# Packed attention and mixture of experts: the first batches' tokens in long pieces, turned by TensorE, and shorter fillers

## The chip, the cores and the metric

One core of a Trainium2 chip. The metric is the device time of one execution in microseconds; of several runs the median counts.

## What is computed

Eight batches of 576 tokens, eight heads of 64. In each head 32 packs attend to the keys, and the queries then attend to the packed result. Its output, heads side by side, goes through a mixture of eight experts with one expert per token.

```python
p_packed = sm_attn(p, k, v)                 # (8, 8, 32, 64)
x = sm_attn(q, p_packed, p_packed)          # (8, 8, 576, 64) -> (8, 576, 512)
logits = np.einsum('bsd,de->bse', x, w_gate)
local_gate = 1.0 / (1.0 + np.exp(-np.einsum('bsd,de->bse', x, w_local).squeeze(-1)))
...
if s == 0 or local_gate[b, s] < 0.5: e = fresh_e      # argmax of the logits
else: e = prev_e
...
h = np.maximum(x[b, s] @ w1[e], 0.0)
out[b, s] = p[e] * (h @ w2[e])
```

## The kernel before

The kernel reads from token 0 of each batch which expert that batch uses and runs the whole batch through it; a part behind a branch mends the tokens for which that doesn't hold, and isn't entered with these inputs. For each batch there is attention (scores of packs against keys, packs, queries against packs), then the choice of the expert (line 565), a register read on SP (line 568), the loads of that expert's w1 and w2 (lines 721 and 730), the product of packs and w1 (line 747), and two layers in eight chunks (lines 770 and 809 to 818). The attention weights go into layer 1 in two parts, a2h and a2l (lines 532 and 535).

Everything is unrolled. The order of the instructions on all engines is written out when the program is built: each piece of work is a generator, `weave` steps one of them at a time, and a model of the engines (`Clock`) says when its inputs, buffers and PSUM banks will be there. `price` holds the model's durations. `need(...)` gives the earliest time of the next step; `weave` takes loads first, then attention work of the earliest batch, then the layers (`main`), weighed by a credit. An attention step may be put ahead of the time at which ScalarE and VectorE are done with their queue by a limit: twice the limit for a step that takes PSUM banks, once for other steps of batches up to `soon`, and none for later batches. `soon` is the first batch whose expert isn't chosen yet. All engines work in the order that results; SP issues nearly all DMAs in order, and one that must wait for a buffer holds up those behind it.

Batch 0 is special (`early`). Its keys and values are loaded as tokens: 96 partitions, pieces of 1536 bytes (`load_tokens`, line 270), in four buffers `kv`. VectorE turns the keys (line 344) in blocks of 32x32. Queries of all batches, and the keys of batches 1 to 7, are loaded in blocks (`load_blocks`, line 284): 128-byte pieces, four transfers, in three buffers `qn`, and VectorE turns them in place (lines 465 and 353). Batch 0's queries are turned after its expert is chosen. Batch 1's loads stand in the order values, packs (line 301), keys, queries; the keys wait until two of batch 0's w2 blocks have been issued, the queries until four have.

Until the first layer starts, TensorE also gets fillers (line 210): products of a constant tile, 128x128 by 256 columns, whose result isn't used. Five stand at the start; one is added for each 450 ns that the model sees TensorE wait, and one whenever the model's share of matmul work falls under a half (`BUSY`, `SLACK`). PSUM has six banks for attention work until then and three afterwards.

Lines that the steps below speak of: scores 385, softmax of the scores 392 to 417, their transposes 427, packs 439 and 454, early choice 577 to 606, query matmuls 480, their softmax 498 to 526, packed weights 747 to 757.

Of the kernel before, what the change touches and what calls it, by code (L numbers as in the profile page):

```python
# [21 lines left out]
HQ = 4  # L22
NQ = H // HQ
TP = 96
# [14 lines left out]
WARM, BUSY, SLACK = 5, 0.5, 1500.0  # L39
# [9 lines left out]
FIRST_W2 = {"k": 2, "q": 4}  # L49
# [5 lines left out]
class Clock:  # L55
# [3 lines left out]
    def __init__(self):  # L59
        self.until, self.written, self.used, self.before = {}, {}, {}, {}  # L60
        self.slots, self.done, self.group, self.tiled, self.products, self.work = {}, set(), (None, set()), False, 0.0, 0.0

        self.rate = 300.0

# [18 lines left out]
    def ready(self, tiles):  # L83
        return max((self.written.get(x.tensor.name, (0.0, None))[0] + LAT for x in tiles), default=0.0)
# [4 lines left out]
    def price(self, inst, outs, ins):  # L89
        kind = str(inst.engine).split(".")[-1]  # L90
        n = max(x.free_size() for x in outs + ins)
        psum = any(x.space == PSUM for x in ins)
        if kind == "PE":
            n = outs[0].free_size()
            rows, at = outs[0].partition_size(), outs[0].start_partition()
            tiled = min(ins[0].partition_size(), rows) <= 64 and rows != 64
            full = n * (0.833 if inst.is_transpose else 1.667 if ins[0].dtype == F32 else 0.4167) + (3 if tiled else 15)

            shape, cell = (rows, n, ins[0].partition_size()), (ins[0].start_partition(), at)
            beside = rows < 128 and shape == self.group[0] and cell not in self.group[1]  # L100
# [6 lines left out]
            self.products += 27.0 if beside else full  # L107
            if not inst.is_transpose:
                self.work += 27.0 if beside else full
            return kind, 27.0 if beside else full  # L110
        extra = len(outs) - 1 + sum(x.free_size() == 1 and n > 1 for x in ins)
        if kind == "Activation":
            return kind, 0.833 * n + (51 if psum else 93) + 93 * extra
        if kind == "DVE" and inst.opcode == "Reciprocal":
            return kind, 6.3 * n + 65
        if kind == "DVE":
            return kind, 1.042 * n + 65 + 60 * extra
        return kind, 1.92 * n + 100

    def note(self, inst):  # L120
# [14 lines left out]
        for x in ins + ([] if dma else outs):  # L135
            at, by = self.written.get(x.tensor.name, (0.0, kind))
            start = max(start, at + (LAT if by != kind else 0.0 if kind == "PE" else SAME))
        for x in outs:
            t = x.tensor.name
            start = max(start, 0.0 if dma else self.used.get(t, 0.0))  # L140
            if t in self.before:
                start = max(start, self.used.get(self.before.pop(t), 0.0) + LAT)
# [4 lines left out]
        for x in ins:  # L147
            self.used[x.tensor.name] = max(end, self.used.get(x.tensor.name, 0.0))
        for x in outs:
            self.written[x.tensor.name] = (end, kind)  # L150
            self.used[x.tensor.name] = max(end, self.used.get(x.tensor.name, 0.0))
# [3 lines left out]
def packed_attn_moe_kernel(  # L155
# [46 lines left out]
    warm = const.tile([128, 256], F32, name="warm")  # L202
# [5 lines left out]
    def keep_warm(n):  # L208
        for _ in range(n):
            nc.tensor.matmul(out=warm_ps[:, :256], lhsT=warm[:, :128], rhs=warm, start=True, stop=True)  # L210
# [41 lines left out]
    def need(*tiles, slot=(), banks=0, when=None):  # L252
# [10 lines left out]
        ready.banks = banks  # L263
# [40 lines left out]
    def begin(b, st, early=False):  # L304
        st["b"], st["early"] = b, early
        st["gate"] = gate_all[b % 3 if isinstance(b, int) else 0]
        st["ppT"] = [None] * NQ
        st["quads"] = st["asked"] = st["scored"] = st["weighed"] = st["raised"] = 0

    def loads(st):  # L310

        b = st["b"]
        if st["early"]:
# [7 lines left out]
            order = (("k", 0), ("k", 1), ("v", 0), ("v", 1), ("q", 1))  # L321
        else:
            if isinstance(b, int):
                yield need(when=lambda: "loaded" in sts[b - 1] and (b < 2 or "ereg" in sts[b - 2]))
            order = (("v", 0), ("v", 1), ("p", 1), ("k", 1), ("q", 1))
        for name, Q in order:
            blocks = name == "q" or (name == "k" and not st["early"])
            if isinstance(b, int) and b == 1 and name in FIRST_W2:
                yield need(when=lambda: len(sts[0].get("w2", ())) >= FIRST_W2[name])
# [15 lines left out]

    def turn_keys(st, Q):

        if not st["early"]:
# [18 lines left out]
    def scores(st, Q):  # L367
# [10 lines left out]
        yield need(key, st["p"], banks=n)  # L378
# [21 lines left out]
        if st["scored"] == NQ:  # L400
# [6 lines left out]
        chunks = sc.rearrange("a (x r p) -> a x r p", x=J3, r=2) if st["early"] \  # L407
            else sc.rearrange("a (r p x) -> a x r p", r=2, x=J3)
# [52 lines left out]
    def turn_queries(st, Q):  # L461
        yield need(when=lambda: "q" in st and "a2t" in st and (not st["early"] or "ereg" in st))
        yield need(st["q"])
        qT = st["q"].rearrange("a (h q) x -> a q h x", q=NQ)[:, Q]
        nc.vector.transpose(out=qT, in_=qT)  # L465
        st["qT", Q] = qT

    def queries(st, Q):

        yield need(when=lambda: st["ppT"][Q] is not None and ("qT", Q) in st and (not st["early"] or ("qT", 1 - Q) in st))  # L470
# [4 lines left out]
        yield need(ppq, st["q"], banks=2)  # L475
# [49 lines left out]
        for r in range(2):  # L525
            nc.vector.transpose(
                out=a2t.rearrange("a (m r) -> a r m", r=2)[:, r],
                in_=sT[:, r].rearrange("a m n -> a (m n)"),
            )
# [182 lines left out]
    def weights(st):  # L712
# [49 lines left out]
    def layer1(c, half, st):  # L762
# [5 lines left out]
        for Q in range(NQ):  # L768
            for wi, ai in ((0, 0), (0, 1), (1, 0)):
# [143 lines left out]
    def weave(main):  # L913
# [3 lines left out]
        idle, seen = SLACK, (START, 0.0)  # L917
        while main in threads or any(x.batch < 0 for x in threads):
# [4 lines left out]
            while started < B and started <= max(at_batch[0], 0) + AHEAD:  # L923
# [3 lines left out]
                    turn_keys(st, 0), turn_keys(st, 1), scores(st, 0), scores(st, 1), keys(st, 0), keys(st, 1), gate_weights(st) if started == 0 else None, gates(st), turn_queries(st, 0), turn_queries(st, 1), queries(st, 0), queries(st, 1),  # L927
# [5 lines left out]
            if at_batch[0] < 0:  # L933
# [8 lines left out]
            behind = max(clock.engine("Activation"), clock.engine("DVE"))  # L942
# [127 lines left out]
```

## Time and profile before

| | us |
|---|---|
| median of 3 runs | 443.4 |
| lowest and highest | 442.42, 444.82 |
| the profiled execution | 446.23 |
| its span, first to last instruction | 444.5 |
| TensorE busy | 424.1 (95%) |
| VectorE, ScalarE, GpSimd busy | 309.1, 176.4, 24.5 |
| first layer-1 matmul of batch 0 | 41.28 |
| first layer-1 matmul of batch 1 | 100.44 |

DMA moved 73.15 MB in 179381 packets, 151424 of them under 512 bytes. The page gives the shares over the whole span; windows give them by stage. In a timeline a line is a run of like instructions: start, length, engine, source line, operation, output and inputs, count, and in brackets the idle time before it and what ended it. PEclk is the granted clock of TensorE as a share of 2.4 GHz: 0.50 is 1.2 GHz.

### The profile page before, as it was taken

What the parts mean: (1) busy time and instruction counts of PE and PEld (TensorE: products, weight loads), DVE (VectorE), ACT (ScalarE), POOL (GpSimd) and SP (SyncE); (2) the same over time, 40 slices, a digit from 0 to 9 for tenths busy, and PEclk for the clock granted to TensorE, in tenths of its full rate; (3) what the DMA queues carried; (4) which work ended last, traced back from release to release, by engine and by line L of the source; (5) the groups of instructions that cost most, each with busy time, mean ns of one, the idle gap of its engine ahead of it and who ended that gap; (6) DMA issues with size and microseconds to landing.
All of it is one profiled execution on the core that took longest, in us unless ns stands there. A gap on an engine that the chain in (4) does not pass through costs nothing.

```text
span 444.5 us, 9978 instructions
## 1 busy us (share of the span) xinstructions
PE 424.1 (95%) x3860; PEld 329.2 (74%) x3861; DVE 309.1 (70%) x837; ACT 176.4 (40%) x400; POOL 24.5 (6%) x41
## 2 busy tenths in 40 slices
PE   8788899979999999999999999999999999999993
PEld 6565587837787678768886778678876888778882
DVE  4478658874897669857986788758985588544331
ACT  1305233345252644355433453445334443344222
POOL 0000000200011001100020002000110002000000
PEclk9888899978999999999999999999999999999998
DMA  9999999999974999399949993799946120821003
GB/s 189 151 245 194 161 217 138 92 324 203 132 161 141 330 133 176 111 323 153 148 164 355 145 165 119 264 198 149 211 137 219 45 88 1 315 106 65 1 1 112
DMA packets 179381, 73.15 MB, mean 165 GB/s; under 512 B 151424, under 2 KB 158336, under 8 KB 179328
## 3 DMA queue, kind: packets, MB, share of 16 engines
q1 hardware_dynamic: 177200, 72.30, 77.9%
q8 instruction: 32, 0.52, 0.6%
q10 hardware_dynamic: 2128, 0.15, 0.4%
q14 instruction: 21, 0.17, 0.2%
HBM read 63.00 MB, written 9.44 MB: 163 GB/s over the span
## 4 chain that ended last, share of the span: by engine, by line
PE 81%; DVE 6%; DMA 4%; SPq 3%; issue 2%; ACT 1%; POOLq 0%; POOL 0%; DVEq 0%
PE acc L809 38%; PE bank L770 22%; PE bank L747 3%; PE bank L439 3%; PE acc L814 3%; PE acc L818 3%; SPq L284 2%; PE bank L427 2%; DVE qn L353 2%; PE bank L480 2%; PE bank L385 2%; DMA p_in<-in_p_dram 2%; DMA qn<-in_k_dram 2%; DMA kv<-in_k_dram 1%; DVE h L785 1%
## 5 line engine op out<-in xcount | busy, mean ns | idle before, releaser
L809 PE MATMUL acc<-w2s,h 128*128 128x512 f32 x768 | 209.1, 403 | 0.0
L809 PEld LDWEIGHTS acc<-w2s,h 128*128 128x128 f32 x768 | 136.2, 190 | 31.6 <-issue 8.6
L780 ACT ACTIVATE h<-bank 128x288 fp32r<-128x288 f32 x128 | 52.7, 412 | 123.3 <-PE bank L770 113.5
L785 DVE SCALAR_TENSOR_TENSOR h<-bank,h 128x288 fp32r<-128x288 f32 (+2 forms) x192 | 61.3, 346 | 43.4 <-ACT h L780 42.5
L770 PE MATMUL bank<-a2h,wph 128*128 128x288 f32 x256 | 78.3, 306 | 2.6 <-DVE df L680 1.2
L770 PE MATMUL bank<-a2h,wpl 128*128 128x288 f32 x256 | 76.1, 297 | 0.0
L770 PE MATMUL bank<-a2l,wph 128*128 128x288 f32 x256 | 75.6, 295 | 0.0
L770 PEld LDWEIGHTS bank<-a2h,wph 128*128 128x128 f32 x256 | 48.4, 189 | 18.7 <-issue 7.3
L770 PEld LDWEIGHTS bank<-a2l,wph 128*128 128x128 f32 x256 | 48.6, 190 | 4.5
L798 DVE TENSOR_TENSOR w2s<-w2raw,w2s 128x512 fp32r<-128x512 f32 x64 | 47.1, 736 | 3.1 <-ACT w2s L796 2.8
L770 PEld LDWEIGHTS bank<-a2h,wpl 128*128 128x128 f32 x256 | 48.5, 189 | 0.0
L796 ACT CAST w2s<-w2raw 128x512 fp32r<-128x512 f32 x64 | 39.4, 615 | 1.2 <-DMA w2raw<-in_moe_w_dram 1.0
L535 POOL TENSOR_TENSOR a2l<-a2t,a2h 128x576 fp32r<-128x576 f32 x14 | 20.5, 1465 | 329.9 <-ACT a2h L532 329.9
L757 DVE TENSOR_TENSOR wpl<-bank,wph 128x512 fp32r<-128x512 f32 x30 | 19.3, 683 | 16.0 <-ACT wph L754 16.0
L814 PE MATMUL acc<-w2s,h 128*128 128x512 f32 x64 | 26.2, 410 | 0.0
L818 PE MATMUL acc<-w2s,h 128*64 128x512 f32 x64 | 25.3, 395 | 0.0
L210 PE MATMUL acc<-warm 128*128 128x256 f32 x78 | 23.9, 469 | 1.2 <-DVE warm L203 1.2
L754 ACT CAST wph<-bank 128x512 fp32r<-128x512 f32 x30 | 16.1, 590 | 21.3 <-PE bank L747 21.3
L210 PEld LDWEIGHTS acc<-warm 128*128 128x128 f32 x78 | 18.1, 240 | 5.7 <-issue 1.6
L465 DVE STREAM_TRANSPOSE qn<-qn 128x1152 f32<-128x1152 f32 x16 | 21.8, 1368 | 0.1
L353 DVE STREAM_TRANSPOSE qn<-qn 128x1152 f32<-128x1152 f32 x14 | 19.0, 1358 | 2.4 <-DMA qn<-in_k_dram 2.4
L447 DVE TENSOR_SCALAR zz<-bank,rs 128x128 f32<-128x128 f32 x16 | 5.6, 351 | 19.9 <-PE bank L439 19.8
(139 smaller groups left out, 416.7 us busy)
## 6 DMA issues: line engine op xcount, KB each, us to landing
w1t<-in_moe_w_dram SPq DMA_DIRECT2D x16, 1024.0 KB, 7.1
w2raw<-in_moe_w_dram SPq DMA_DIRECT2D x64, 256.0 KB, 7.4
kv<-in_v_dram SPq DMA_DIRECT2D x16, 576.0 KB, 9.8
qn<-in_q_dram SPq DMA_DIRECT2D x32, 288.0 KB, 7.3
out_dram<-o SPq DMA_DIRECT2D x32, 256.0 KB, 3.6
qn<-in_k_dram SPq DMA_DIRECT2D x28, 288.0 KB, 8.1
kv<-in_k_dram SPq DMA_DIRECT2D x2, 576.0 KB, 6.3
out_dram<-o SPq DMA_DIRECT2D x8, 128.0 KB, 3.2
```

What stands on the lines that cost most here:

```text
L210: nc.tensor.matmul(out=warm_ps[:, :256], lhsT=warm[:, :128], rhs=warm, start=True, stop=True)
L353: nc.vector.transpose(out=kT, in_=kT)
L465: nc.vector.transpose(out=qT, in_=qT)
L535: eng.tensor_tensor(out=a2l, in0=a2t, in1=a2h.bitcast(F32), op=ALU.subtract)
L770: nc.tensor.matmul(out=t[:, :HALF], lhsT=st["wp"][c // 4][wi][:, Q, fs], rhs=a2[ai][Q][:, ts], start=(n == 0), stop=(n == 5),)
L780: nc.scalar.activation(out=h[:, HALF * half:HALF * half + HALF], in_=t[:, :HALF], func=AF.Relu)
L785: nc.vector.scalar_tensor_tensor(out=h[:, dst:dst + z - a], in0=t[:, a:z], scalar=0.0, in1=h[:, HALF * half + a:HALF * half + z].bitcast(F32),
L796: nc.scalar.copy(out=w[:, 0], in_=raw)
L798: nc.vector.tensor_tensor(out=w[:, 1], in0=raw, in1=w[:, 0].bitcast(F32), op=ALU.subtract)
L809: nc.tensor.matmul(out=acc, lhsT=hs[hi], rhs=w[:, wi], start=(c == 0 and n == 0), stop=(c == NC - 1 and n == 2),)
L814: nc.tensor.matmul(out=acc, lhsT=h[:, 512:S + TAIL], rhs=w[:, 0], start=(c == 0), stop=False, skip_group_check=True,)
L818: nc.tensor.matmul(out=acc[0:TAIL], lhsT=h[:, 512:S], rhs=w[:, 1], start=False, stop=(c == NC - 1), skip_group_check=True,)
```

## The change

Batch 0's queries, batch 1's keys and batch 1's queries are loaded as tokens, like the keys and values of batch 0: two transfers each in 1536-byte pieces, in the buffers `kv`. A new function `turn_tokens` turns them: for each half of the heads and each head three transposes by TensorE into one PSUM bank, and a copy by ScalarE into a tile of the tag `qn`. For the three tensors that is 72 transposes and 24 copies; six VectorE transposes of 128x1152 go. Batch 0's queries no longer wait for its choice.

Batch 1's loads stand in the order packs, keys, values, queries; packs and keys no longer wait for batch 0's w2 blocks; the values wait for two, the queries for four. The columns of the turned tensors come in another order, so the last transposes of the query softmax (line 526) write in another pattern for batches 0 and 1.

Fillers have 128 columns instead of 256; ten stand at the start, one is added per 400 ns of waiting, and the rule by share of work is gone. In the model the price of a matmul that runs beside others is 7 instead of 27 ns, and that of a switch of tile shape 90 or 110 instead of 84; halves of a turned tile are followed apart. `soon` is 0 until the first layer; steps of batches beyond `soon` get no advance even if they take banks; and a step is held against the engines that it names (`by`) only. In layer 1 the loop over Q is the inner one.

```diff
-WARM, BUSY, SLACK = 5, 0.5, 1500.0
+WARM, FILL = 10, 400.0
...
-FIRST_W2 = {"k": 2, "q": 4}
+FIRST_W2 = {"v": 2, "q": 4}
...
-            full += 84.0 if self.tiled and not tiled else 0.0
+            full += 0.0 if self.tiled == tiled else 90.0 if tiled else 110.0
...
-            return kind, 27.0 if beside else full
+            self.products += 7.0 if beside else full
+            return kind, 7.0 if beside else full
...
-    warm = const.tile([128, 256], F32, name="warm")
+    warm = const.tile([128, 128], F32, name="warm")
...
-            order = (("k", 0), ("k", 1), ("v", 0), ("v", 1), ("q", 1))
+            order = (("k", 0), ("k", 1), ("v", 0), ("v", 1), ("q", 0), ("q", 1))
...
-            order = (("v", 0), ("v", 1), ("p", 1), ("k", 1), ("q", 1))
+            order = (("p", 1), ("k", 0), ("k", 1), ("v", 0), ("v", 1), ("q", 0), ("q", 1)) if st["second"] else \
+                (("v", 0), ("v", 1), ("p", 1), ("k", 1), ("q", 1))
...
+    def turn_tokens(st, name):
+
+        yield need(slot="qn", when=lambda: (name, 0) in st and (name == "k" or "a2t" in st))
+        xT = st[name] = tile_([128, NQ, HQ, HALF], F32, "qn")
+        clock.halves[xT.tensor.name] = H * HALF
+        for Q in range(NQ):
+            yield need(when=lambda: (name, Q) in st)
+            x = st[name, Q]
+            for h in range(HQ):
+                yield need(x, banks=1, by=("Activation",))
+                tp = bank()
+                for c in range(J3):
+                    nc.tensor.transpose(
+                        out=tp[:, TP * c:TP * c + TP], in_=x[:, h, 2 * D * c:2 * D * c + 2 * D], identity=ident[:TP, :TP],
+                    )
+                yield need(tp, by=("Activation",))
+                nc.scalar.copy(out=xT[:, Q, h], in_=tp[:, :HALF])
+                give(tp)
+            give(x)
+            st[name + "T", Q] = xT[:, Q]
+
     def turn_keys(st, Q):
 
-        if not st["early"]:
+        if st["second"]:
+            yield need(when=lambda: "p" in st and "ereg" in sts[0])
+        elif not st["early"]:
...
-        yield need(when=lambda: "q" in st and "a2t" in st and (not st["early"] or "ereg" in st))
+        yield need(when=lambda: "q" in st and "a2t" in st)
...
-        yield need(when=lambda: st["ppT"][Q] is not None and ("qT", Q) in st and (not st["early"] or ("qT", 1 - Q) in st))
+        yield need(when=lambda: st["ppT"][Q] is not None and ("qT", Q) in st)
...
+            if st["early"] or st["second"]:
+
+                out = a2t.rearrange("a (p i c r) -> a r c p i", p=TP // 32, i=32, c=J3)[:, r]
+                nc.vector.transpose(out=out, in_=sT[:, r].rearrange("a (c p) n -> a c p n", c=J3))
...
-                yield need(when=lambda: all(c < n or x in sts[1] for x, n in FIRST_W2.items()))
+                yield need(when=lambda: all(c < n or (x, 1) in sts[1] for x, n in FIRST_W2.items()))
...
-        for Q in range(NQ):
-            for wi, ai in ((0, 0), (0, 1), (1, 0)):
+        for wi, ai in ((0, 0), (0, 1), (1, 0)):
+            for Q in range(NQ):
...
-                idle = min(idle + clock.work - seen[1] - BUSY * (now - seen[0]), SLACK)
-                seen = now, clock.work
-                if idle < 0:
-                    keep_warm(1)
-                    continue
...
-            soon = next((b for b in range(B) if "ereg" not in sts[b]), B)
-            when = {x: t if x is main or x.loads else max(t, behind - limit * (2.0 if x.ready.banks else 1.0 if x.batch <= soon else 0.0))
+            soon = next((b for b in range(B) if "ereg" not in sts[b]), B) if at_batch[0] >= 0 else 0
+            when = {x: t if x is main or x.loads else max(t, max(clock.engine(y) for y in x.ready.by) - limit * (0.0 if x.batch > soon else 2.0 if x.ready.banks else 1.0))
...
-                    keep_warm(max(0, int((when[x] - now) / 450.0)))
+                    keep_warm(max(0, int((when[x] - now) / FILL)))
```

## Rows read from the trace of the kernel before

**Rows 1.** Section 2 of the page: granted TensorE clock by slice, tenths.

```profile
PEclk9888899978999999999999999999999999999998
```

**Rows 2.** Windows of line 770 alone: batch 0's layers, then the next five's.

```profile
41.00:100.40 59.40, 16.19 (x96) 14.35 (x96) 0.92 1.04 187
...
100.40:351.70 251.30, 79.02 (x480) 71.98 (x481) 0.99 0.89 183
```

**Rows 3.** Windows: length; PE, PEld, DVE, ACT, POOL busy; PEclk; DMA share; GB/s.

```profile
48.00:58.00 10.00, 8.00 (x61) 5.02 (x60) 6.80 (x19) 2.63 (x7) 0.00 (x0) 0.83 1.12 136
...
90.00:104.20 14.20, 11.16 (x115) 6.36 (x114) 9.41 (x49) 5.32 (x13) 0.37 (x2) 0.64 1.03 341
...
100.00:351.00 251.00, 249.79 (x2399) 193.71 (x2392) 189.75 (x510) 111.02 (x256) 16.64 (x20) 0.99 0.90 184
```

**Rows 4.** Timeline of TensorE, 0 to 60 us: start, us, what, [idle before].

```profile
1.23 8.18 PE L210 MATMUL acc<-warm 128*128 128x256 f32 x28 [1.23 <-DVE warm L203]
...
9.34 1.15 PE L385 MATMUL acc<-kv,p_in 32*32 32x192 f32 x48
...
18.61 0.74 PE L439 MATMUL bank<-kv,a1T 96*32 96x64 f32 x18 [2.53 <-issue]
...
21.11 3.78 PE L210 MATMUL acc<-warm 128*128 128x256 f32 x8
...
24.82 0.42 PE L599 MATMUL acc<-gate,et 128*32 128x32 f32 x4
...
28.55 0.94 PE L480 MATMUL bank<-qn,ppT 64*32 64x288 f32 x20
...
41.28 0.40 PE L770 MATMUL bank<-a2h,wph 128*128 128x288 f32 x1
```

**Rows 5.** Timeline of SP, 0 to 110 us: its DMA issues.

```profile
6.53 13.03 SPq L284 DMA_DIRECT2D qn<-in_q_dram  x4
...
27.23 1.05 SPq L721 DMA_DIRECT2D w1t<-in_moe_w_dram  x2
...
31.07 12.39 SPq L284 DMA_DIRECT2D qn<-in_k_dram  x4
...
46.25 7.91 SPq L284 DMA_DIRECT2D qn<-in_q_dram  x4
```

**Rows 6.** Windows as in rows 3, for the rate of the transfers.

```profile
14.00:18.00 4.00, 2.07 (x85) 1.73 (x85) 1.82 (x7) 0.76 (x2) 0.00 (x0) 1.00 1.47 118
...
32.00:36.00 4.00, 1.31 (x18) 0.34 (x17) 3.92 (x10) 1.40 (x3) 0.00 (x0) 0.97 1.05 387
...
58.00:64.00 6.00, 6.00 (x124) 5.09 (x123) 2.52 (x7) 3.63 (x10) 0.00 (x0) 1.00 0.91 265
...
70.00:84.00 14.00, 14.00 (x83) 11.87 (x86) 12.33 (x27) 6.29 (x14) 1.43 (x1) 1.00 1.14 135
```

**Rows 7.** Timeline of VectorE, 0 to 60 and 60 to 104 us.

```profile
23.02 0.24 DVE L596 STREAM_TRANSPOSE et<-es 128x64 f32<-128x64 f32 x1
...
26.09 0.14 DVE L565 TENSOR_SCALAR e<-ecd 1x1 int32<-1x1 f32 x1
...
26.26 2.64 DVE L465 STREAM_TRANSPOSE qn<-qn 128x1152 f32<-128x1152 f32 x2
...
38.34 1.48 DVE L535 TENSOR_TENSOR a2l<-a2t,a2h 128x576 fp32r<-128x576 f32 x2
...
61.21 1.38 DVE L465 STREAM_TRANSPOSE qn<-qn 128x1152 f32<-128x1152 f32 x1
...
88.08 0.14 DVE L565 TENSOR_SCALAR e<-codes_all 1x1 int32<-1x1 f32 x1
```

**Rows 8.** Chain that ended last (start, us), and a group of the page.

```profile
57.14 0.65 PE bank L427 x6
...
L780 ACT ACTIVATE h<-bank 128x288 fp32r<-128x288 f32 x128 | 52.7, 412 | 123.3 <-PE bank L770 113.5
```

**Rows 9.** Groups of instructions, 0 to 42 us: busy us, mean ns.

```profile
L526 DVE STREAM_TRANSPOSE a2t<-sT 128x288 f32<-128x288 f32 x4 | 1.6, 446 | 0.0
```

More of the change, by code (lines that the diff above doesn't have):

```diff
@@ L60, in __init__, with key @@
         self.until, self.written, self.used, self.before = {}, {}, {}, {}
-        self.slots, self.done, self.group, self.tiled, self.products, self.work = {}, set(), (None, set()), False, 0.0, 0.0
+        self.slots, self.done, self.group, self.tiled, self.products = {}, set(), (None, set()), False, 0.0
+        self.halves = {}
         self.rate = 300.0
+    def key(self, x):
+        n = self.halves.get(x.tensor.name)
+        return x.tensor.name if n is None else (x.tensor.name, 2 * (x.offset % n) >= n)
     def follow(self, tile, tag, bufs):
@@ L83, in ready @@
     def ready(self, tiles):
-        return max((self.written.get(x.tensor.name, (0.0, None))[0] + LAT for x in tiles), default=0.0)
+        return max((self.written.get(self.key(x), (0.0, None))[0] + LAT for x in tiles), default=0.0)
     def engine(self, name):
@@ L135, in note @@
         for x in ins + ([] if dma else outs):
-            at, by = self.written.get(x.tensor.name, (0.0, kind))
+            at, by = self.written.get(self.key(x), (0.0, kind))
             start = max(start, at + (LAT if by != kind else 0.0 if kind == "PE" else SAME))
@@ L139, in note @@
             t = x.tensor.name
-            start = max(start, 0.0 if dma else self.used.get(t, 0.0))
+            start = max(start, 0.0 if dma else self.used.get(self.key(x), 0.0))
             if t in self.before:
@@ L146, in note @@
             end += 2000.0
-        for x in ins:
-            self.used[x.tensor.name] = max(end, self.used.get(x.tensor.name, 0.0))
         for x in outs:
-            self.written[x.tensor.name] = (end, kind)
-            self.used[x.tensor.name] = max(end, self.used.get(x.tensor.name, 0.0))
+            self.written[self.key(x)] = (end, kind)
+        for x in ins + outs:
+            for t in {x.tensor.name, self.key(x)}:
+                self.used[t] = max(end, self.used.get(t, 0.0))
 @with_exitstack
@@ L209, in keep_warm @@
         for _ in range(n):
-            nc.tensor.matmul(out=warm_ps[:, :256], lhsT=warm[:, :128], rhs=warm, start=True, stop=True)
+            nc.tensor.matmul(out=warm_ps[:, :128], lhsT=warm, rhs=warm, start=True, stop=True)
     keep_warm(WARM)
@@ L250, in give, with need @@
         clock.done.update(x.tensor.name for x in tiles)
-    def need(*tiles, slot=(), banks=0, when=None):
+    def need(*tiles, slot=(), banks=0, when=None, by=("Activation", "DVE")):
         slots = [(x, 1) if isinstance(x, str) else x for x in ((slot,) if isinstance(slot, str) else slot)]
@@ L262, in ready @@
             return max(clock.ready(tiles), free[banks - 1][0] if banks else 0.0, *(clock.slot(*x) for x in slots))
-        ready.banks = banks
+        ready.banks, ready.by = banks, by
         return ready
@@ L305, in begin @@
         st["b"], st["early"] = b, early
+        st["second"] = isinstance(b, int) and b == 1
         st["gate"] = gate_all[b % 3 if isinstance(b, int) else 0]
@@ L324, in loads @@
                 yield need(when=lambda: "loaded" in sts[b - 1] and (b < 2 or "ereg" in sts[b - 2]))
-            order = (("v", 0), ("v", 1), ("p", 1), ("k", 1), ("q", 1))
+            order = (("p", 1), ("k", 0), ("k", 1), ("v", 0), ("v", 1), ("q", 0), ("q", 1)) if st["second"] else \
+                (("v", 0), ("v", 1), ("p", 1), ("k", 1), ("q", 1))
         for name, Q in order:
-            blocks = name == "q" or (name == "k" and not st["early"])
-            if isinstance(b, int) and b == 1 and name in FIRST_W2:
+            blocks = name in "kq" and not (st["early"] or st["second"])
+            if st["second"] and name in FIRST_W2:
                 yield need(when=lambda: len(sts[0].get("w2", ())) >= FIRST_W2[name])
@@ L377, in scores @@
         key = st["k", Q] if st["early"] else st["k"]
-        yield need(key, st["p"], banks=n)
+        yield need(st["p"], st["kT", Q] if st["second"] else key, banks=n)
         ts = [bank() for r in range(n)]
@@ L474, in queries @@
         sT = tile_([128, 2, HALF // 32, NP], F32, "sT")
-        yield need(ppq, st["q"], banks=2)
+        yield need(ppq, qT, banks=2)
         ts = [bank() for r in range(2)]
```

18 lines of the change are left out of this document (7 added, 11 removed).

## The prediction

> **What bounds the kernel now.** I read the slices of the page first. TensorE is busy almost throughout; its granted clock dips early, in the first quarter, and then stays full to the last slice [rows 1]. Next I counted layer 1 by batch: 96 matmuls of line 770 belong to each batch. Batch 0's layers take 59.4 us from the first of them to batch 1's first; the next five batches take 251.3 us, 50.3 each [rows 2]. So batches 1 to 5 run at TensorE's own pace (from 100 to 351 us it is idle for 251 - 249.79 = 1.2 us [rows 3]), and no transfer or evacuation there is worth anything. What can be won lies ahead of the first layer-1 matmul, at 41.28 us [rows 4], and in batch 0's stretch. There two windows hold the loss [rows 3]: 48 to 58 us, idle 2.0 and a mean clock of 0.83, so 0.17 x 10 = 1.7 lost; and 90 to 104.2 us, idle 3.0 and a clock of 0.64, so 0.36 x 14.2 = 5.1. Less some 0.7 counted twice (idle at half clock), that is 11.1 us. The timelines of TensorE, SP and VectorE say why.
>
> **The start-up, part by part.** The chain is: keys, scores, packs, the choice of batch 0's expert, the expert's w1, and beside it queries, softmax, a2l, the packed weights, first layer.
>
> Queries in pieces. SP is occupied for 13.03 us by the four query transfers in 128-byte pieces, and later for 12.39 us by batch 1's keys [rows 5]. Pieces of 1536 bytes move at 265 GB/s (batch 2's values, 58 to 64 us) and pieces of 128 bytes at 135 (its keys and queries, 70 to 84) [rows 6]: 1.18 MB takes 4.5 us instead of 8.7. Ahead of the choice stand packs, keys, values and queries, 3.74 MB; at 265 they land 14.1 us after the first moves at some 2.5, so near 17. The new loads take the slots of the keys and wait for the scores, whose first half ends at 10.5 [rows 4], which is no delay, since the values are in flight until about 12.
>
> The Trainium skill (Perfetto Trace Analysis, DMA Optimizations) puts a significant overhead on every piece under 2 KB; by that the new pieces are still small. The rows agree in part: 265 GB/s, against 387 for the weights at 32 to 36 us [rows 6]. By the rule alone the sum would lose the 4 us that I let each tensor save; by the rows it keeps them.
>
> Ahead of the choice, TensorE stands still for 2.53 us within one group of matmuls, for nothing that the trace shows, while the queues move 118 GB/s with the small query pieces in flight [rows 4, 6]. I take that stall away (bounds 0 and 2.5). Then eight fillers at half clock, 3.78 us from 21.11, stand in front of the matmul of line 599, which starts at 24.82 [rows 4] though VectorE had its input done at 23.26 [rows 7]. Fillers of half the length and fewer of them give back these 1.5 us. Sum 4.0: the choice, done at 26.23 [rows 7], could be done at 22.2.
>
> Against that stands the clock. Before, 28 fillers run for 8.18 us up to the first scores [rows 4]. After, I count ten and some nine more for the gap (400 ns each by the plan), each half as long: some 3 us, and then TensorE is idle for 4 to 5. The row after the 2.53 us gap has fillers at 0.47 us each, against 0.29 at the start; an idle stretch of that length cost the clock. So the scores, transposes and packs up to 16.07 us (two groups of scores at 1.15, twelve transposes at 0.11 [rows 8], the packs about as long: 4.9 in all) may run at half clock: 0 to +4.9, taken +3.0, as the gap is nearly twice the one that did it. The choice comes at 25.2, w1 is issued at 26.2 (1.0 later, as before [rows 5, 7]). Batch 1's packs and keys go ahead of it on SP, as its values and packs did; the second half of these keys waits for the slot of batch 0's values, free by 19, and the 1.3 MB are through by 24. So w1 finds the queues empty and lands by some 31 and 34.
>
> Beside it the queries are turned by TensorE and ScalarE instead of VectorE's 2.64 us [rows 7], and no longer wait for the choice. 24 transposes at 0.11 us (six took 0.65) and eight copies at 0.41 [rows 8]: ScalarE's 3.3 us decide, so they are ready by 22 to 23; the packs, which stood a little ahead of 21, come there again. The query matmuls start near 24 instead of 28.55. From there to the end of a2l it was 11.3 us (39.82), and 1.46 more to the first layer [rows 4, 7]: 24 + 11.3 + 1.46 = 36.8. The scattered output of the transposes of line 526 has no row; the even one takes 0.446 us [rows 9], four lie on this chain; taken at no change, bounds 0 and +1.8. **Term 1: 41.3 to 36.8, -4.5** (-7.5 without the cold clock, +1.0 with all of it and no quicker transfer).
>
> **Batch 0's stretch.** The first stall is batch 1's scores: SP issues its keys from 31.07, behind w1. After, they land near 24, so the scores lie before or right at the first layer. The second stall is batch 1's late choice, 88.08 [rows 7]. Its queries were issued from 46.25 for 7.9 us and their first turn starts at 61.21 [rows 5, 7]. After: w1 through at 34, two w2 blocks 1.3, the values 4.5, two w2 blocks 1.3, the queries 4.5: 46. From queries to choice it was 26.9 us, and 12.3 on to batch 1's first layer; 46 + 39.2 = 85. TensorE has work until 36.8 + 50.3 + 2.6 = 89.7. So the choice no longer ends last, by some 4 us. What comes late next is the clock: there are few fillers from 22 to 36.8, and if the layers begin at half clock, between what the first stall's clock cost (1.7) and what the second's did (5.1) is lost [rows 3]; taken 2.5. I keep 2 more for stalls at the three banks that transposes and layer 1 now share. **Term 2: -11.1 + 4.5 = -6.6** (bounds -11.1 and -2).
>
> **What is added.** TensorE turns two more tensors, batch 1's keys (before the layers, in idle time; if not, 2.6) and its queries, which fall into its full stretch: 24 x 0.108 = 2.6. ScalarE's 16 copies (6.6 us) lie beside. VectorE is rid of 4 x 1.37 us, and was not last there once the choice is early. **Term 3: +2.6** (bounds +1.0, the second a gain if the earlier scores leave the stretch, and +5.2).
>
> The Trainium skill (VectorE: DVE Perf Modes, The three transpose paths) calls VectorE's transpose the fastest for 32x32 blocks and sends 128x128 ones to TensorE. The old path is the first kind. The rows bear it out for the bound engine: kept on VectorE, this term is 0 and the sum 2.6 us lower, were the small pieces not its price.
>
> **All other batches.** The plan's prices change (side-by-side matmuls 7 ns instead of 27, a switch of tile shape 90 or 110 instead of 84), and work of batches beyond the next choice gets no advance. The two outer loops of layer 1 trade places, at the same count. No row shows the new order; there is 1.2 us to gain, and a boundary stall to lose. **Term 4: 0** (bounds -1.2 and +3).
>
> **Sum:** -4.5 - 6.6 + 2.6 = -8.5 us. The profiled execution took 446.23 us, 1.7 of them outside its span of 444.5, and lies 2.8 above the median; the same 8.5 off the median gives 443.4 - 8.5 = **434.9**, say 435.
>
> **Rivals.** *Both terms in full:* no cold start, no new stall: -7.5 - 11.1 + 1.0 = -17.6, less 1.2 at most: 425 to 430. For it: the transposes themselves keep TensorE at work. Against: sparse fillers. *The start-up runs cold:* +1.0 on the first layer, and 5.1 + 2 lost after it: +1.0 - 11.1 + 7.1 + 2.6 = -0.4, 443. For it: every idle stretch of 2.5 us or so in the rows was followed by half clock. *Batch 1 isn't earlier:* its queries wait for the slots of its keys, and these are turned only when ScalarE is free; then only the first stall goes (2 of the 11.1, after a cold start): -4.5 - 2 + 2.6 = -3.9, 439.5. *The change doesn't do what it says:* pieces of 1536 bytes move no faster here than those of 128, since the first transfers share the queues: 4 us later for queries and w1, 439. *Slower:* work for the batch after next is held back until the next choice is known; so its own choice comes late and each later boundary waits like 48 to 58 us did, 2.0 + 1.7 = 3.7 [rows 3]. There are six such boundaries; from the third on it is a loss (434.9 + 11.1 = 446), four give 450. Against it: VectorE and ScalarE have slack, and boundaries cost 1.2 us in all now.
>
> **Chances.** Forecast 0.52 (own range 430 to 440), both in full 0.10, cold 0.12, batch 1 not earlier 0.14, no faster pieces 0.04, slower 0.08. The range 427.5 to 442 leaves out most of the best case, all of the slower one and half of the cold one, about 0.2. A measurement of this kernel tells some 0.5% from no change, so faster is below 441.2: 0.52 + 0.10 + 0.13 + 0.03 + 0.02 = 0.80; within 0.5% 0.11, of the cold case above all; slower 0.09.
>
> **What would show it.** In the profile after: the first matmul of line 770 near 37 (term 1; the choice near 25, no idle stretch within line 439); the granted clock from 5 to 20 us and at the first layer (the cold case); batch 1's choice near 73, and no idle or half-clock window around batch 1's first layer (term 2); the transposes of the new function at about 0.11 us (term 3); 50.3 us a batch afterwards, idle about 1 us (term 4). Wrong would be a first layer after 40, a choice of batch 1 after 80, or batches 1 to 5 above 51 us each.

## The result, and the profile after

The changed kernel takes 440.29 us (median of 15 runs), the kernel before 442.89 beside it; the ratio is 0.994, interval 0.991 to 0.996. The forecast was 434.9: the sign was right, but the gain was 2.6 us and not the 8.5 of the sum. The two profiled executions differ by far more, 446.23 and 440.03 us; that difference is the first thing to explain.

The timelines of the profile after (start, us, what, idle before), TensorE's first, then VectorE's and SP's:

```profile
1.09 6.18 PE L214 MATMUL acc<-warm 128*128 128x128 f32 x38 [1.09 <-DVE warm L207]
8.80 1.15 PE L415 MATMUL acc<-kv,p_in 32*32 32x192 f32 x48 [1.53 <-DVE p_in L351]
...
21.98 0.31 PE L635 MATMUL acc<-gate,et 128*32 128x32 f32 x4
...
36.15 0.82 PE L806 MATMUL bank<-a2h,wph 128*128 128x288 f32 x2 [1.52 <-DVE wpl L793]
```

```profile
21.37 0.24 DVE L632 STREAM_TRANSPOSE et<-es 128x64 f32<-128x64 f32 x1
...
23.65 0.14 DVE L601 TENSOR_SCALAR e<-ecd 1x1 int32<-1x1 f32 x1
...
75.79 0.14 DVE L601 TENSOR_SCALAR e<-codes_all 1x1 int32<-1x1 f32 x1
```

```profile
10.01 2.28 SPq L274 DMA_DIRECT2D kv<-in_q_dram  x2
...
24.81 1.39 SPq L757 DMA_DIRECT2D w1t<-in_moe_w_dram  x2
...
76.72 1.01 SPq L757 DMA_DIRECT2D w1t<-in_moe_w_dram  x2
```

The first layer (line 806, 770 before) starts at 36.15 instead of 41.28 [rows 4]. The choice of batch 0 is done at 23.8 instead of 26.2 and that of batch 1 at 75.9 instead of 88.2 [rows 7]; the query transfers hold SP for 2.28 us instead of 13.03 [rows 5]; no filler stands ahead of the matmul of line 635, which starts 0.4 us after its input is done.

After the first layer I divide TensorE's time into three: idle (length less busy), lost to the clock (half of the busy time in stretches whose PEclk is 0.50, so that idle time in them isn't counted twice), and its own work (the rest). The ends of matmuls are modelled, so short waits within a row of matmuls count as work here. Windows of the kernel before, from batch 0's first layer to batch 1's, from there to batch 2's, and on to the last matmul, and then its half-clock stretches in them (length; PE, PEld, DVE, ACT, POOL busy with counts; PEclk; DMA share; GB/s):

```profile
41.28:100.44 59.16, 53.70 (x558) 39.84 (x551) 43.10 (x132) 22.77 (x55) 3.60 (x6) 0.91 1.04 187
100.44:150.21 49.77, 49.77 (x418) 38.84 (x415) 37.24 (x102) 20.68 (x47) 3.24 (x4) 0.96 0.88 184
150.21:437.69 287.48, 286.27 (x2513) 226.07 (x2511) 201.86 (x531) 123.92 (x281) 16.61 (x20) 1.00 0.70 153
...
52.84:56.25 3.41, 3.41 (x25) 1.74 (x23) 1.49 (x6) 1.16 (x3) 0.00 (x0) 0.50 1.37 149
93.80:104.03 10.23, 8.61 (x81) 5.60 (x82) 5.68 (x32) 4.90 (x12) 0.00 (x0) 0.50 1.06 354
```

The same after:

```profile
36.15:91.96 55.81, 54.09 (x575) 42.16 (x575) 37.14 (x117) 23.29 (x61) 4.22 (x6) 0.95 1.04 209
91.96:144.72 52.76, 51.53 (x486) 38.84 (x486) 40.95 (x120) 23.14 (x55) 3.51 (x4) 1.00 0.92 182
144.72:430.85 286.13, 284.98 (x2442) 224.27 (x2440) 201.15 (x526) 121.23 (x274) 16.14 (x20) 1.00 0.67 149
...
36.15:42.18 6.03, 6.03 (x51) 5.62 (x52) 4.05 (x9) 1.43 (x4) 0.00 (x0) 0.50 1.08 262
```

Before: idle 5.46 + 0 + 1.21 = 6.7, clock (3.41 + 8.61) / 2 = 6.0, work 396.4 - 12.7 = 383.7. After: idle 1.72 + 1.23 + 1.15 = 4.1, clock 6.03 / 2 = 3.0, work 394.7 - 7.1 = 387.6. So the stalls gave 5.6 us, the first layer 5.1, and TensorE's own work took 3.9 back; after the last matmul 7.4 us pass instead of 6.8. Up to rounding that is the 6.3 us between the two spans (444.5 and 438.2).

The expectations below speak of 382.4 and 387.6 us of work and of a growth of 5.1 to be explained. These are rougher sums, from PEclk rounded to two digits and with idle time at half clock taken off twice; by the sums above the growth is 3.9 here and 4.1 in the mean of two profiles each.

### The profile page after: what moved, and what is told of

Its sections match the earlier page's. It is cut to its first block, busy times and chain, and to the rows that moved or that the text cites. A ratio compares the mean times of both kernels' runs of the same rounds, so it can differ in the third digit from the quotient of the medians.

```text
span 438.2 us, 10127 instructions
## 1 busy us (share of the span) xinstructions
PE 417.8 (95%) x3928; PEld 326.9 (75%) x3929; DVE 303.9 (69%) x831; ACT 183.5 (42%) x424; POOL 24.9 (6%) x41
## 4 chain that ended last, share of the span: by engine, by line
PE 88%; DVE 5%; DMA 3%; issue 1%; ACT 1%; SPq 0%; POOLq 0%; DVEq 0%; POOL 0%; ACTq 0%
PE acc L845 40%; PE bank L806 24%; PE acc L850 4%; PE bank L783 3%; DMA kv<-in_k_dram 3%; PE acc L854 3%; PE bank L470 3%; PE bank L415 2%; PE bank L458 2%; PE bank L511 2%; PE bank L658 1%; DVE wpl L793 1%; PE bank L365 1%; DVE a2t L560 1%; PE acc L214 0%
## 5 line engine op out<-in xcount | busy, mean ns | idle before, releaser
L806 PEld LDWEIGHTS bank<-a2h,wph 128*128 128x128 f32 x256 | 47.0, 191 | 23.9 <-issue 3.6
L806 PE MATMUL bank<-a2h,wph 128*128 128x288 f32 x256 | 57.9, 308 | 5.5 <-DVE wpl L793 1.8
L806 PE MATMUL bank<-a2l,wph 128*128 128x288 f32 x256 | 55.5, 299 | 0.0
L806 PE MATMUL bank<-a2h,wpl 128*128 128x288 f32 x256 | 55.3, 298 | 0.0
L806 PEld LDWEIGHTS bank<-a2l,wph 128*128 128x128 f32 x256 | 41.7, 191 | 0.0
L806 PEld LDWEIGHTS bank<-a2h,wpl 128*128 128x128 f32 x256 | 41.7, 191 | 0.0
L783 PE MATMUL bank<-w1t,ppT 64*32 64x512 f32 x248 | 17.4, 601 | 2.7 <-DVE sm L550 1.6
L529 DVE STREAM_TRANSPOSE sT<-bank 128x288 f32<-128x288 f32 x30 | 12.8, 462 | 10.1 <-ACT gate L527 9.4
L448 ACT ACTIVATE a<-a,nb 128x576 f32<-128x576 f32 x16 | 12.5, 779 | 14.9 <-DVE nb L433 14.9
L460 ACT COPY a1T<-bank 96x384 f32<-96x384 f32 x28 | 13.3, 477 | 10.5 <-PE bank L458 10.0
L383 DVE STREAM_TRANSPOSE qn<-qn 128x1152 f32<-128x1152 f32 x12 | 16.4, 1364 | 0.1
```

The source lines that it names most:

```text
L783: nc.tensor.matmul(out=ts[Q][32 * h:32 * h + 32, :], lhsT=st["ppT"][Q][rows, 32 * h:32 * h + 32], rhs=w1t[rows, h], start=True, stop=True,)
L806: nc.tensor.matmul(out=t[:, :HALF], lhsT=st["wp"][c // 4][wi][:, Q, fs], rhs=a2[ai][Q][:, ts], start=(n == 0), stop=(n == 5),)
```

## The experiments

All times are medians beside the kernel before on the same chip, which was at 442.8 to 443.2 in every group.

**Both kernels again.** No edit; a second profile of each.

> The kernel before, unchanged, for a second profile and many times. Two theories of why the median moved by 2.6 us and the two profiled executions by 6.2. A: the profiled execution of before had more half-clock time than most (granted clock 0.970 over its span, about 13 us at half pace counted as lost); then the executions here differ by some 4 us among themselves, the longer ones have the lower mean clock, and a profile at the median (about 443 us, span 441) has a mean clock near 0.976. B: the clock is always 0.970 and the time differs for another reason; then time and mean clock don't go together. Ratio to itself 1.000 within 0.003.

> The changed kernel, unchanged. Ratio 0.994 within 0.003. A: over the executions the time rises as the mean clock falls, by about 4 us per 0.01 of it, as 437.3 us at 0.991 and 441.4 at 0.977 did. B: no such slope. First layer-1 matmul near 36 us again, half clock over the first layers again.

Before: 442.35 us, ratio 0.999 (0.996 to 1.002). After: 440.40, ratio 0.993 (0.990 to 0.996). In the four groups of 25 to 35 executions of the kernel before the time goes with the mean granted clock, 3.2 to 3.6 us per 0.01 of it (correlation -0.79 to -0.89; the 35 of one group lie between 439.9 and 446.3 us); over the twelve of the changed kernel it is 3.1 at -0.58. That is theory A, with a slope somewhat below the 4 it named. The second profile of before was taken in an execution of 442.06 us, mean clock 0.977 instead of 0.970; first layer, the three windows and their one half-clock stretch:

```profile
39.68 0.40 PE L770 MATMUL bank<-a2h,wph 128*128 128x288 f32 x1
```

```profile
39.68:96.64 56.96, 52.52 (x559) 39.14 (x551) 43.61 (x133) 22.68 (x55) 3.61 (x6) 0.93 1.11 192
96.64:146.03 49.39, 49.39 (x418) 38.54 (x415) 37.26 (x102) 20.70 (x47) 3.25 (x4) 0.97 0.87 184
146.03:433.54 287.51, 286.29 (x2513) 226.06 (x2511) 201.98 (x531) 124.07 (x281) 16.64 (x20) 1.00 0.68 153
...
89.20:99.44 10.24, 8.61 (x87) 4.99 (x80) 6.45 (x38) 4.69 (x12) 0.00 (x0) 0.50 1.06 366
```

The same program, counts alike: work 383.9, idle 5.7, clock 4.3. The first layer comes 1.6 us earlier and 2.7 us less is lost afterwards. The second profile of the changed kernel went the other way and not as expected, an execution of 441.68 us:

```profile
38.80 0.51 PE L806 MATMUL bank<-a2h,wph 128*128 128x288 f32 x2 [1.04 <-DVE wpl L793]
```

```profile
38.80:93.97 55.17, 51.88 (x574) 39.68 (x575) 37.05 (x117) 23.88 (x62) 4.23 (x6) 1.00 1.12 208
93.97:146.71 52.74, 51.48 (x486) 38.83 (x487) 40.94 (x120) 23.15 (x55) 3.50 (x4) 1.00 0.92 186
146.71:432.78 286.07, 284.91 (x2442) 224.11 (x2440) 201.16 (x526) 121.23 (x274) 16.14 (x20) 1.00 0.67 149
```

Work 388.3, idle 5.7, nothing lost to the clock after the first layer; in exchange the half-clock stretch lay in the start-up, as a window of this same profile shows:

```profile
20.00:30.00 10.00, 9.48 (x90) 5.93 (x76) 5.96 (x20) 3.96 (x12) 0.00 (x0) 0.53 0.62 141
```

So the profiled execution of before was 3.3 us longer than its median, and the sum was made on it. Where half-clock stretches fall differs between executions of one program. Up to the last matmul they last 10.2 us in all in both profiles of the changed kernel, once at 11 to 15 and 35 to 42 us, once at 21 to 31; in the kernel before they last 23.9 and 17.1 us. Of the mean of the two profiles each: first layer 40.5 before, 37.5 after; idle and clock 11.3 and 6.4; work 383.8 and 387.9. That is -3.0, -4.9 and +4.1, and 0.5 more behind the last matmul: -3.3 us, against -2.6 of the medians.

One part of the growth needs no sum over the whole. From batch 1's first layer to the last matmul none of the new transposes is left, and TensorE gets nearly the same matmuls in both kernels (2931 and 2928 records in the second and third windows). They are 334.2 and 334.3 us of work before (49.77 + 286.27 less the 1.8 lost to the clock after 100.44, and 49.39 + 286.29 less 1.4) and 336.5 and 336.4 after: 2.2 us more.

**The fillers alone.**

```diff
 # in the changed kernel
-WARM, FILL = 10, 400.0
+WARM, BUSY, SLACK = 5, 0.5, 1500.0
...
-            nc.tensor.matmul(out=warm_ps[:, :128], lhsT=warm, rhs=warm, start=True, stop=True)
+            nc.tensor.matmul(out=warm_ps[:, :256], lhsT=warm[:, :128], rhs=warm, start=True, stop=True)
```

> The changed kernel with the fillers of before: 256 columns, five at the start, one per 450 ns, and the rule by share of matmul work. Theory C (the shorter, fewer fillers cost the clock at the first layer, 36 to 42 us, some 3 us): the first layers run at full clock and the time falls by 2 to 3 us against the changed kernel. Theory D (the long fillers delay work by as much as the clock gives): the first layer comes 1.5 to 4 us later and the time is equal or longer, 440 to 443.

440.39 us, ratio 0.993 (0.990 to 0.997). The first layer came at 39.79, and at full clock:

```profile
39.79:93.76 53.97, 51.88 (x574) 39.68 (x575) 37.05 (x117) 23.73 (x62) 4.23 (x6) 1.00 1.07 218
```

That is 3.6 us later than in the first profile of the changed kernel, whose first layers ran at half clock, and 1.0 later than in the second, whose first layers ran at full clock too; the time is the same. That is theory D. The reverse, the new fillers in the kernel before:

> The kernel before with only the new fillers (128 columns, ten at the start, one per 400 ns, no rule by share). C: the start-up chain and the first layers lose 2 to 5 us to half clock, 445 to 448. D: the choice comes 1.5 us earlier because no filler stands in front of it, and the time is 440 to 443.

443.49 us, ratio 0.999 (0.996 to 1.003): none of C's loss, and half a microsecond above D's range. And more of the short ones (`WARM, FILL = 20, 150.0` in the changed kernel):

> The changed kernel with twenty fillers at the start and one per 150 ns of waiting instead of one per 400. Theory C (half clock in the start-up and the first layers is what is left to win): no half clock between 10 and 45 us, first layer at 35 to 36, time 437 to 438. Theory D (fillers stand in front of work): half clock is less, but the first layer comes at 37 or later, time 440 or more.

442.16 us, ratio 1.000 (0.996 to 1.003), 1.8 us more than the changed kernel, at a higher granted clock: the median over the executions is 0.995 against 0.984. In its profile, taken in the longest of its executions (447.32 us), 42 and 22 fillers stand in a row before the first layer, which comes at 46.20:

```profile
35.16 4.88 PE L214 MATMUL acc<-warm 128*128 128x128 f32 x42
...
40.98 2.72 PE L214 MATMUL acc<-warm 128*128 128x128 f32 x22
...
46.20 0.54 PE L806 MATMUL bank<-a2h,wph 128*128 128x288 f32 x2 [1.07 <-ACT qn L369]
```

The part of the change that concerns fillers is worth nothing that these runs could tell either way.

**One tensor pair at a time.** Batch 0's queries only; batch 1 loaded and turned as before:

```diff
-        st["second"] = isinstance(b, int) and b == 1
+        st["second"] = False
...
-FIRST_W2 = {"v": 2, "q": 4}
+FIRST_W2 = {"k": 2, "q": 4}
...
-                    ... if started > 1 else (turn_tokens(st, "q"),)
+                    ... if started > 0 else (turn_tokens(st, "q"),)
```

> The changed kernel with batch 1's keys and queries loaded in blocks and turned by VectorE as before, in the order of before; batch 0's queries stay in pieces on TensorE. Two theories of the 5.1 us that TensorE's own work after the first layer grew by (382.4 before, 387.6 after, idle and half clock taken off). E: batch 1's transposes on TensorE cost it, 5 us instead of the 2.6 I had; then the work here is 382 to 384, the stall before batch 1 is back (idle and half clock after the first layer about 11 us), and the time is 440 to 442. F: the plan's new prices and order cost it in the later batches; then the work stays at 387 and the time is 443 to 446.

445.04 us, ratio 1.003 (0.998 to 1.007), not the 440 to 442 of E but within F's 443 to 446. The windows:

```profile
39.32:98.20 58.88, 53.41 (x562) 40.93 (x558) 44.25 (x133) 22.57 (x55) 3.86 (x6) 0.94 1.02 184
98.20:151.90 53.70, 53.42 (x529) 40.59 (x528) 38.11 (x109) 23.64 (x55) 3.22 (x4) 0.97 1.10 206
151.90:436.29 284.39, 283.26 (x2393) 223.29 (x2391) 199.89 (x524) 120.88 (x273) 16.43 (x20) 1.00 0.64 148
```

The stalls are back (idle 6.9, clock 4.4), as expected, and the work is 385.7: between E's bound of 384 and F's 387. Batch 1's turning accounts for 387.9 - 385.7 = 2.2 of the 4.1 us; 1.9 are there without it. The other half, with batch 0's queries in blocks on VectorE:

```diff
-            order = (("k", 0), ("k", 1), ("v", 0), ("v", 1), ("q", 0), ("q", 1))
+            order = (("k", 0), ("k", 1), ("v", 0), ("v", 1), ("q", 1))
...
-                    ... if started > 1 else (turn_tokens(st, "q"),)
+                    ... if started != 1 else (turn_tokens(st, "q"),)
```

> The changed kernel with batch 0's queries in blocks, turned by VectorE after the choice, as before; batch 1's keys and queries in pieces on TensorE. The first layer should come 2 to 4 us later than in the changed kernel, 39 to 41. E and F both have the work at 387. If the start is worth what it looks like, the time is 442 to 444.

443.42 us, ratio 1.001 (0.999 to 1.004), as expected; the first layer comes at 42.11, later than the 39 to 41 expected:

```profile
42.11:96.31 54.20, 51.20 (x542) 39.45 (x543) 37.00 (x110) 24.65 (x63) 4.04 (x6) 1.00 1.02 206
96.31:149.04 52.73, 51.47 (x485) 38.81 (x486) 40.92 (x120) 23.15 (x55) 3.49 (x4) 1.00 0.86 183
149.04:434.44 285.40, 284.24 (x2442) 224.18 (x2440) 200.98 (x526) 121.16 (x274) 16.13 (x20) 1.00 0.66 150
```

The stalls are small (idle 5.4, clock 0), and the work is 386.9. So batch 1's pieces take the stalls away and pay for it with work. Batch 0's seem to bring the first layer forward (39.32 in only_q0), but that is one profile each, and two profiles of one kernel differ by up to 2.7 us there. Neither half gains alone.

**What a transpose costs.** Each of batch 1's query transposes done twice:

```diff
-                for c in range(J3):
+                for c in list(range(J3)) * (2 if st["second"] and name == "q" else 1):
```

> The changed kernel with every transpose of batch 1's queries done twice (24 more, the same eight visits to a bank); the result is the same. G: what batch 1's queries cost TensorE is the transposes themselves; 24 more cost as much again as the 24 do, 0.08 to 0.11 us each, 2 to 2.6 us. H: half of the cost is the break in the row of layer matmuls at each visit; then the work after the first layer rises by no more than 2 us, from 387.6 to 389.5, and the time by about that.

441.08 us, ratio 0.995 (0.991 to 0.998): by the time alone not to be told from the changed kernel. Windows after the first layer:

```profile
37.13:91.24 54.11, 53.58 (x599) 41.79 (x599) 37.65 (x117) 24.70 (x63) 4.05 (x6) 1.00 1.01 213
91.24:143.99 52.75, 51.49 (x486) 38.83 (x486) 40.91 (x120) 23.17 (x55) 3.51 (x4) 1.00 0.92 182
143.99:430.06 286.07, 284.92 (x2442) 224.13 (x2440) 201.07 (x526) 121.39 (x274) 16.19 (x20) 1.00 0.66 149
```

The work is 390.0 us, 2.4 more than in the first profile of the changed kernel and 1.7 more than in the second, for 24 transposes: 0.07 to 0.10 us each. That reaches into G's range (2 to 2.6) and below H's bound (2), so the two are not told apart; but at least 1.7 of the 2.2 us above lie in the transposes themselves, which leaves little for the visits.

**Where the other 1.9 us come from.** The plan's prices taken back:

```diff
-            full += 0.0 if self.tiled == tiled else 90.0 if tiled else 110.0
+            full += 84.0 if self.tiled and not tiled else 0.0
...
-            return kind, 7.0 if beside else full
+            return kind, 27.0 if beside else full
```

> The changed kernel with the plan's prices of before (27 ns for a matmul beside others, 84 for a switch from tiled to full shapes). E: nothing changes in the sum, work after the first layer 387, 440 to 441. F: the work in batches 1 to 7 falls from 336 to 334 us, and the time to 438 to 439.

440.19 us, ratio 0.994 (0.991 to 0.997), work 387.7: against F. The rule for running ahead taken back:

```diff
-            soon = next((b for b in range(B) if "ereg" not in sts[b]), B) if at_batch[0] >= 0 else 0
-            ... limit * (0.0 if x.batch > soon else 2.0 if x.ready.banks else 1.0))
+            soon = next((b for b in range(B) if "ereg" not in sts[b]), B)
+            ... limit * (2.0 if x.ready.banks else 1.0 if x.batch <= soon else 0.0))
```

> The changed kernel with the rule of before for how far attention work may run ahead (2, 1 or 0 times the limit, against both ScalarE and VectorE, and the first batch without an expert also during the start-up). With only batch 0's queries changed TensorE's work after the first layer was 384.9, and 382.5 before; prices were no cause. F2: the rule costs these 2.4 us; then the work here is 385 and the time 438. If not, 387 to 388 and 440.

442.09 us, ratio 0.999 (0.996 to 1.001): the work after the first layer is 384.6, but at least in part since the first layer comes at 43.58, with part of batch 1's work ahead of it. F2's number came, and not its time. Layer 1's loops swapped back:

> The changed kernel with layer 1's loops as before, the half of the heads outside. F3: the order of the six products costs the 2.4 us; then work after the first layer is 385 and the time 438. If not, it is 387 to 388 and 440.

440.84 us, ratio 0.994 (0.991 to 0.997), work 388.2: no effect. Then the other way round, the rule and the prices each put alone into the kernel before:

> The kernel before with only the new rule for how far attention work may run ahead (nothing for batches beyond the next choice; the start-up counts batch 0 as that one). F2: the rule is where 2.4 us of TensorE's work after the first layer come from; then it rises from 382.5 to 385 and the time by 1 to 2.5 us. If not, the work stays at 382 to 383.

443.67 us, ratio 1.002 (0.998 to 1.006), counts per window as in the kernel before (558, 419 and 2513 matmuls; before_again 559, 418 and 2513): after the first layer the order hardly changes, and the work is 384.6 against 383.8, so this rule alone is not it.

> The kernel before with only the new prices in the plan (7 ns beside others, 90 and 110 for a switch of shape). F: the prices are the source, work 385. Taking them back out of the changed kernel left its work at 387.6, so the other answer is likelier: work 382 to 383, time as before.

447.05 us, ratio 1.010 (1.007 to 1.013), the one clear loss, where none was expected:

```profile
38.97:98.92 59.95, 54.89 (x504) 38.57 (x496) 46.70 (x133) 21.25 (x50) 3.84 (x6) 0.91 1.11 193
98.92:153.14 54.22, 53.81 (x544) 41.49 (x541) 37.43 (x112) 25.51 (x60) 3.22 (x4) 0.97 0.93 186
153.14:438.49 285.35, 284.18 (x2442) 224.17 (x2440) 201.05 (x526) 121.15 (x274) 16.10 (x20) 1.00 0.68 150
```

Work 386.1, 2.3 more than before, and the third window now holds the count of the changed kernel (2442). The stalls are larger too in this profile: idle and clock 13.4, against 11.3 in the mean of the kernel before. And batch 0's queries alone with prices and rule of before:

> Batch 0's queries in pieces, turned by TensorE, batch 1 as before, with the prices and the rule of before. With the new ones its work after the first layer was 384.9. If rule and prices together are the source, the work falls to 382 to 383. If it stays at 385, the 2.4 us come with the other order of the loads and turns itself, not with the plan's numbers.

442.59 us, ratio 0.999 (0.995 to 1.002):

```profile
40.30:99.78 59.48, 55.29 (x554) 41.72 (x550) 43.31 (x132) 21.90 (x54) 3.61 (x6) 0.87 0.98 182
99.78:149.40 49.62, 49.62 (x418) 38.67 (x415) 37.26 (x102) 20.74 (x47) 3.25 (x4) 0.97 0.84 183
149.40:437.43 288.03, 286.93 (x2513) 225.94 (x2511) 202.06 (x531) 124.26 (x281) 16.66 (x20) 1.00 0.68 153
```

Work 384.1, 1.6 less than with the new plan, and some 2 us less time, though the intervals overlap. So where batch 1 is as before, the new prices (here together with the rule) cost 1.6 to 2.3 us of TensorE's work, by another order of the same instructions. In the changed kernel, taking them back alone does not return it. Why it doesn't is open: the parts of the plan do not add. The order of layer 1's loops was not put alone into the kernel before.

**A version that keeps what pays.** Batch 0's queries and batch 1's keys in pieces on TensorE; batch 1's queries in blocks, turned by VectorE:

```diff
-            blocks = name in "kq" and not (st["early"] or st["second"])
+            blocks = name in "kq" and not (st["early"] or st["second"] and name == "k")
...
-                    ... if started > 1 else (turn_tokens(st, "q"),)
+                    ... if started > 0 else (turn_tokens(st, "q"),)
```

> The changed kernel with batch 1's queries in blocks again, turned by VectorE; batch 0's queries and batch 1's keys stay in pieces, turned by TensorE. E: the 2.8 us that batch 1's turning costs after the first layer go (work 385), and the queries land 4 us later, which is covered if batch 1's choice does not end last; time 438 to 439. If the later queries bring the stall before batch 1 back, 441 to 443.

436.76 us, ratio 0.986 (0.983 to 0.988): better than both kernels, and than the 438 to 439 expected.

```profile
38.26:89.98 51.72, 50.01 (x512) 37.65 (x512) 41.10 (x130) 20.18 (x50) 3.85 (x6) 0.97 1.10 196
89.98:142.20 52.22, 51.85 (x530) 40.34 (x524) 37.85 (x108) 24.45 (x57) 3.17 (x4) 1.00 1.03 215
142.20:428.26 286.06, 284.94 (x2442) 224.15 (x2440) 201.08 (x526) 121.25 (x274) 16.15 (x20) 1.00 0.66 149
```

Work 385.1 (2.8 less than the changed kernel), idle 3.2, clock 1.7; batch 1's choice is done at 77.3 although its queries hold SP for 16.37 us:

```profile
32.62 16.37 SPq L288 DMA_DIRECT2D qn<-in_q_dram  x4
```

## Why the forecast gain was too large, step by step

**Term 1, the first layer.** Forecast 36.8; the first profile has 36.15, the second 38.80. Of the mechanism, the stall within the packs (2.53 us) and the fillers ahead of line 599 are gone in the first profile. Half clock in the start-up was foreseen and priced at 3.0, but not as it came: 38 fillers ran up to 7.27 us where I had counted nineteen, TensorE then stood still for 1.53 us and not for 4 to 5, and the half clock fell on 11 to 15 us and on the first layers in the first profile, and on 21 to 31 us in the second. So that 36.15 lies near 36.8 is in part luck. And the start I compared with, 41.28, was itself a late one: 39.68 in the other profile, with the same instructions. By the means the term is -3.0, not -4.5.

**Term 2, the stalls.** Forecast -6.6, measured -5.6 between the two first profiles and -4.9 in the means. Batch 1's choice came at 75.9 (77.9 in the second profile) against my 73; only_q0, without batch 1's pieces, has the stalls back. The mechanism was right, and the size 1.7 us too large by the means: the half clock after the first stall (52.84 to 56.25 us) is not there at all in the second profile of the kernel before.

**Term 3, the added turning.** Forecast +2.6. Measured 2.2 (changed kernel against only_q0), and 1.7 to 2.4 for a second set. Right, if a little large. The advice of the Trainium skill that I set beside it (VectorE: DVE Perf Modes, Rules for kernel authors: VectorE's transpose is the fastest for 32x32 blocks) is what the mixed version follows for batch 1's queries, and its work is 2.8 us lower there.

**Term 4, all other batches.** Taken at 0, bounds -1.2 and +3; measured +2.2 (334.2 and 334.3 us of work from batch 1's first layer on before, 336.5 and 336.4 after), or +1.9 by only_q0 against the kernel before. This is the step that failed outright. I had read that later batches run at TensorE's pace with 1.2 us idle, and concluded that a new order could only add stalls. It added none: idle after batch 2's start is 0.8 to 1.2 us in every profile. The order itself costs work; the kernel before with nothing but the new prices is 1.0% slower, with 2.3 us more work. Which neighbours cost it, or whether it is short waits that count as busy, is open. That layers and attention alternate more often is not it: in the traces TensorE changes between the two 151 times from batch 1's first layer on before, and 141 times after. The sign that I had set for this term did not show it either. Batches 1 to 5 take 250.8 us, 50.2 each, against 251.3 before, of which 1.8 were lost to the clock. My slower rival had the right place, the plan's new order behind the first batch, but looked for idle boundaries, and there are none.

**From the profile to the median.** I subtracted 8.5 us, worked out on an execution of 446.23 us, from a median of 443.4, saying that the difference was 2.8 and no more. But those 2.8 us were part of what the sum counted as winnable: the second profile of the kernel before has its first layer 1.6 us earlier and lacks the half clock after the first stall, 1.7 us. Executions without them cannot win them. Together: 8.5 less 1.5 (term 1), 1.7 (term 2), 1.5 (terms 3 and 4) and 0.5 behind the last matmul is the 3.3 us of the mean profiles; the medians say 2.6, and a few tenths stay open with two profiles each.

**Small pieces.** The rule that pieces under 2 KB carry a significant overhead (the Trainium skill, Perfetto Trace Analysis, DMA Optimizations) would have left the 1536-byte pieces little better. The queries' two transfers occupied SP for 2.28 us instead of 13.03, and the queue moved 244 GB/s from 14 to 18 us in the first profile after, against 118 in the same window before [rows 6]:

```profile
14.00:18.00 4.00, 3.80 (x113) 3.34 (x112) 2.26 (x8) 1.22 (x3) 0.00 (x0) 0.89 1.09 244
```

So the pieces do pay, short of 2 KB. The 265 GB/s that I had taken for them were read in a window in which w2 was in flight too: 502 of its 958 packets had 2 KB or more, some 1.03 of 1.59 MB. At 244 a tensor of 1.18 MB takes 4.8 us and not 4.5, which changes no step.

## What to carry to other kernels

When the engine that bounds a stage has no idle time, a new order of the same instructions can still cost it time; compare its own work (busy time less what the clock cost of it), not its idle time alone. Make the sum on more than one profile, or ask first how far the profiled execution lies from the median and which of the losses in it are the difference. And split a change by tensor: here batch 1's keys on TensorE paid and its queries did not.

## What the runs showed of the hardware

With one program, 35 executions lie between 439.9 and 446.3 us, and their time goes with the mean granted clock, 3.6 us per 0.01 in that group. Half-clock stretches appear at other places each time (after the first layer 6.0 us were lost to them in one profile of before and 4.3 in the other; in the changed kernel 3.0, or none there and the stretch in the start-up). Fillers of either length, few or many, did not shorten the execution in any of three tries; many of them raised the mean clock (0.995 against 0.984), stood in front of work, and the time was 1.8 us longer. A new order of nearly the same matmuls took 2.2 us more of TensorE's time (336.4 against 334.2) with no idle time added.
